# Moving the places where h's two parts and the stacks begin in their SBUF buffers

## The chip, the core and the metric

The kernel runs on one core of one Trainium2 chip. The metric is the device time of one execution in microseconds (us); lower is better. The core has five engines that run their own instruction queues and wait for each other through semaphores: TensorE (PE, with its weight loads shown apart as PEld), VectorE (DVE), ScalarE (ACT), GpSimd (POOL) and SyncE (SP), which here issues the DMAs.

## What is computed

Inputs are `x` of 4 batches x 12416 rows x 128 features, 32 learned rows `inducing`, and three weight matrices of a gated feed-forward layer with 1536 hidden units. The reference, cut to what matters:

```
def mab(q, kv):                       # attention, one head
    a = softmax(scale * q @ kv.T)
    return a @ kv
h   = mab(inducing for each batch, x) # 4 x 32 x 128
y   = mab(x, h)                       # 4 x 12416 x 128
g   = y @ w_gate
out = (g * sigmoid(g)) * (y @ w_val) @ w_out
```

Since y is a weighted mean of 32 rows, y @ w_gate is computed as attention weights times (h @ w_gate), so a contraction over 32 rows takes the place of one over 128.

## The kernel before

The feed-forward part is most of the work. For each batch the rows are cut into 25 column tiles: the first has 512 columns, then come twelve of 512 and twelve of 480. For every column tile 12 tiles t of 128 hidden units follow each other; such a pair of column tile and t is a slot, 300 to a batch. In a slot the kernel does this:

- `front`: two matmuls (L668, L669) multiply the batch's weights `tw` with the column tile's `stack`, a 128-row matrix in which the attention weights stand twice as a high part and twice as a low part, into two PSUM banks `gv`. ACT applies SiLU to one (L671, tile `silu`), DVE multiplies with the other (L676), which gives h, in the SBUF tile `h`, or for t = 1, 5 and 9 in the PSUM bank itself.
- `split`, one slot later: h is rounded to fp32r as `h_hi` (L685; by ACT, for t = 11 by DVE), and the rest `h_lo` = h - h_hi is written (L687; by POOL, for t = 1, 5 and 9 by DVE).
- `back`, some 5 to 10 slots later: three matmuls add h_hi times the low part of w_out (L701), h_hi times its high part (L702) and h_lo times the high part (L703) into the PSUM bank `o`. After t = 11 DVE copies `o` to `ob` (L710) and a DMA writes it out.

So PE's queue repeats L668, L669, L701, L702, L703, one round for each slot. The very first column tile of batch 0 is an exception: its h is one part, and L699 multiplies it. Between the slots stand the steps of the attention of this and the next batch, at slots set by a plan; the whole order is written out in the program.

In the first 65 us or so ACT and POOL also make the weights: L187 (POOL) adds the halves of a weight word, L190 (ACT) rounds w_out to `wo_hi`, L193 (POOL) writes `wo_lo`. These have the same form as L685 and L687.

Where things lie in a partition of SBUF, in the built program before the change: there are 11 buffers for h_hi, 10 for h_lo, 3 for h, 2 for silu, each 2048 bytes long and back to back, and every one begins 32 bytes past a multiple of 2048. The 3 buffers of the stack are also back to back and begin 928 bytes past a multiple of 2048; `wo_hi`, `wo_lo`, `tw` and `wgv_sb` begin 1504 bytes past one. Where L193 and L190 read their operands differs: `tw` lies 1504 bytes past a multiple of 2048, as wo_hi and wo_lo do; the pieces in `s_all` and `xn_sb` lie 1952 past one, 448 bytes off. The remainder of a start by 2048 bytes is called its phase below.

Of the kernel before, what the change touches and what calls it, by code (L numbers as in the profile page):

```python
# [9 lines left out]
F32 = mybir.dt.float32  # L10
F32R = mybir.dt.float32r
# [7 lines left out]
P = 128  # L19
# [13 lines left out]
NF = len(FC)  # L33
W = 32 * max(CH)
WF = 32 * max(FC)
NT = DFF // P
SCALE = 1.0 / math.sqrt(C)


COLS = [(0, 0)] + [(q, j) for q in range(1, NF) for j in range(NG)]  # L40
SLOTS = len(COLS) * NT
NXT = 4
# [66 lines left out]
def induced_set_attention_then_swiglu(ctx: ExitStack, tc: tile.TileContext, xt, xn, ind, wgv, wo, out):  # L109
# [8 lines left out]
    stp = ctx.enter_context(tc.tile_pool(name="stp", bufs=NST))  # L118
# [30 lines left out]
    def wcol(k, t):  # L149
        at = WP * (t // 2) + 2 * P * k + P * (t % 2)  # L150
        return slice(at, at + P)
# [46 lines left out]
    def attention(b, one, xn0=None, xt0=None):  # L198

        st = Batch()  # L200
# [14 lines left out]
        def fblocks(q):  # L215
            return FC0[q], FC0[q] + FC[q]
# [200 lines left out]
        def sl2(b0, b1):  # L417
            return st.s2[:, b0:b1, :]
# [32 lines left out]
        def aT(q):  # L451
            st.at[q] = sgl.tile([P, WF], F32, name="aT")
            nc.vector.transpose(out=st.at[q][:, :32 * FC[q]], in_=sl2(*fblocks(q)).rearrange("p t m -> p (t m)"))

        def a_hi(q, eng=nc.vector.tensor_copy):
            st.ah[q] = sgl.tile([P, WF], F32R, name="a_hi")
            eng(out=st.ah[q][:, :32 * FC[q]], in_=st.at[q][:, :32 * FC[q]])  # L457

        def a_lo(q, eng):
            st.al[q] = sgl.tile([P, WF], F32R, name="a_lo")  # L460
            n = 32 * FC[q]
            eng.tensor_sub(out=st.al[q][:, :n], in0=st.at[q][:, :n], in1=st.ah[q][:, :n].bitcast(F32))  # L462

        def stack(u):
            if u not in st.stack:
                st.stack[u] = stp.tile([P, WF], F32R, name="stack")
            return st.stack[u]

        def spread(u):

            q, j = COLS[u]
            n = 32 * FC[q]
            sk = stack(u)
            for g in range(4):
                src = (st.ah, st.al)[g % 2][q]
                for jj in range(NG) if q == 0 else (j,):
                    c0 = n * jj if q == 0 else 0
                    nc.sync.dma_start(out=sk[32 * g:32 * g + 32, c0:c0 + n].bitcast(F32), in_=src[32 * jj:32 * jj + 32, :n].bitcast(F32))
# [41 lines left out]
        def z7(h):  # L520
            nc.scalar.copy(out=zhalf(stack(0), h), in_=zhalf(st.zps, h))

        def z8(h):
            nc.vector.scalar_tensor_tensor(out=zhalf(stack(0), h), in0=zhalf(stack(0).bitcast(F32), h), scalar=odd, in1=zhalf(st.zps, h), op0=ALU.mult, op1=ALU.add)
# [8 lines left out]
    def post(st, q, eng, base, ready=0):  # L533

        f = st.f
        steps = [(0, lambda: f["sum2"](q)), (1, lambda: f["rec2"](q)), (2, lambda: f["norm2"](q, eng)),
                 (5, lambda: f["aT"](q)), (7, lambda: f["a_hi"](q)), (9, lambda: f["a_lo"](q, eng))]
        tiles = [u for u, (p, j) in enumerate(COLS) if p == q]
        return [(base + d, g) for d, g in steps] + [
            (max(base + 12, ready + NT * (u - NST + 1) + 3), lambda u=u: f["spread"](u)) for u in tiles]  # L540

    def plan(st, p):
# [6 lines left out]
        def clear(slot):  # L549

            while slot % NT in p["TABU"]:
                slot += 1
# [41 lines left out]
        for q in range(NF):  # L594
            first = [u for u, (p, j) in enumerate(COLS) if p == q][0]
            s += post(st, q, nc.gpsimd, SLOTS + NT * (first - NST) + 2, SLOTS)
        return sorted(s, key=lambda x: x[0])
# [53 lines left out]
    hip = ctx.enter_context(tc.tile_pool(name="hip", bufs=BF[2]))  # L651
    lop = ctx.enter_context(tc.tile_pool(name="lop", bufs=BF[3]))
# [5 lines left out]
    def front(st, b, c, t):  # L658
        u = Tile()
        q, j = COLS[c]  # L660
        u.b, u.q, u.j, u.t = b, q, j, t
        n = u.n = WF if q == 0 else 32 * FC[q]

        u.whole = b == 0 and c == 0
        rhs = st.stack[c][:, :n]
        u.g = ps_gv.tile([P, 512], F32, name="gv")
        u.v = ps_gv.tile([P, 512], F32, name="gv")
        nc.tensor.matmul(out=u.g[:, :n], lhsT=st.w[:, wcol(0, t)], rhs=rhs, start=True, stop=True)  # L668
        nc.tensor.matmul(out=u.v[:, :n], lhsT=st.w[:, wcol(1, t)], rhs=rhs, start=True, stop=True)  # L669
        s = sip.tile([P, WF], F32, name="silu")  # L670
        nc.scalar.activation(out=s[:, :n], in_=u.g[:, :n], func=AF.Silu)  # L671
        if u.whole:
            u.h = hip.tile([P, WF], F32, name="h_hi")
        else:
            u.h = u.v if t in DVE_TILES else hp.tile([P, WF], F32, name="h")
        nc.vector.tensor_mul(out=u.h[:, :n], in0=u.v[:, :n], in1=s[:, :n])  # L676
        return u

    def split(u):
        if u.whole:  # L680
            return
        n = u.n
        u.hi = hip.tile([P, WF], F32R, name="h_hi")
        u.lo = lop.tile([P, WF], F32R, name="h_lo")
        (nc.vector.tensor_copy if u.cast_dve else nc.scalar.copy)(out=u.hi[:, :n], in_=u.h[:, :n])  # L685
        eng = nc.vector if u.t in DVE_TILES or u.last else nc.gpsimd
        eng.tensor_sub(out=u.lo[:, :n], in0=u.h[:, :n], in1=u.hi[:, :n].bitcast(F32))  # L687
# [3 lines left out]
    def back(u):  # L691
# [5 lines left out]
        if u.whole:  # L697
            k = t % (WP // P)
            nc.tensor.matmul(out=o[:, :n], lhsT=pieces[f"o{t // (WP // P)}"].w[:, P * k:P * k + P], rhs=u.h[:, :n], start=(t == 0), stop=(t == NT - 1))  # L699
        else:  # L700
            nc.tensor.matmul(out=o[:, :n], lhsT=wo_lo[:, ws], rhs=u.hi[:, :n], start=(t == 0), stop=False)  # L701
            nc.tensor.matmul(out=o[:, :n], lhsT=wo_hi[:, ws], rhs=u.hi[:, :n], start=False, stop=False)  # L702
            nc.tensor.matmul(out=o[:, :n], lhsT=wo_hi[:, ws], rhs=u.lo[:, :n], start=False, stop=(t == NT - 1))  # L703
        if t == NT - 1:
# [11 lines left out]
    for b in range(B):  # L716
# [12 lines left out]
        for slot in range(SLOTS):  # L729
            c, t = slot // NT, slot % NT  # L730
            u = front(cur, b, c, t)
            u.cast_dve = t in CAST
            u.last = b == B - 1 and slot == SLOTS - 1
            if wait:
                split(wait[0])
                pend.append(wait.pop(0))
            wait.append(u)
            if slot in bursts:
                u.cast_dve = True
                split(u)  # L740
                pend.append(wait.pop(0))
            for a in (cur, nxt):
                while a is not None and a.steps and a.steps[0][0] <= slot:
                    a.steps.pop(0)[1]()
            ahead = min(ahead + 1 / RAMP, HI) if nxt is not None and slot < last_burst else max(ahead - 1 / RAMP, SKEW)
            if slot in bursts:
                ahead = SKEW
            while len(pend) + len(wait) > ahead:
                back(pend.pop(0))
# [3 lines left out]
    for u in wait:  # L753
        split(u)
# [39 lines left out]
```

## Time and profile before

| | |
|---|---|
| median of 3 runs | 1501.12 us (1500.82 to 1503.07) |
| the profiled execution: its time, its span | 1499.66 us, 1497.6 us |
| mean granted TensorE clock | 0.999 of full speed |
| busy: PE, PEld, DVE, ACT, POOL | 1475.7, 1166.2, 1214.6, 1283.6, 1208.5 us |

The span runs from the first to the last instruction; 2.1 us of the profiled time lie outside of it. PE's busy time is a union of matmuls that overlap in the record, since they are pipelined and their ends are modelled; the distance from one matmul's start to the next one's start tells the pace.

### The profile page before, as it was taken

Reading aid. Unit: us, or ns where it says so; the run is one execution under the profiler, and the core shown is the slowest. Engines: PE = TensorE matmul, PEld = TensorE weight load, DVE = VectorE, ACT = ScalarE, POOL = GpSimd, SP = SyncE. Lnnn points to the kernel's source line nnn. Section 1 sums busy time; section 2 is a strip of 40 time slices with the busy share of each in tenths; the row PEclk is TensorE's granted clock in tenths of the full one; section 3 lists DMA queues with packets and bytes.
Section 4 is the critical chain, followed back from the end, with each engine's and each line's share of the span. In section 5 each row is a group of like instructions: output and inputs, shape, how many; then the busy total and the mean of one; then the engine's idle time right before and its main releaser. Section 6 shows DMA issues by size and latency. Waiting matters only on the chain.

```text
span 1497.6 us, 24960 instructions
## 1 busy us (share of the span) xinstructions
PE 1475.7 (99%) x7465; PEld 1166.2 (78%) x7465; DVE 1214.6 (81%) x2083; ACT 1283.6 (86%) x2389; POOL 1208.5 (81%) x995
## 2 busy tenths in 40 slices
PE   8899999999999999999999999999999999999999
PEld 5576777788887776788887777678888887888887
DVE  6788778878888778788888878878878878878877
ACT  5787888789898887889989888789898898898897
POOL 1588767878898778788888877978889888888887
PEclk9999999999999999999999999999999999999999
DMA  9026322221133333121114324221111111111110
GB/s 369 23 94 187 135 96 94 79 61 56 40 109 120 122 125 112 46 67 37 40 44 131 125 87 156 78 69 48 41 40 35 38 41 41 33 41 39 41 40 20
DMA packets 50822, 119.80 MB, mean 80 GB/s; under 512 B 11392, under 2 KB 28288, under 8 KB 50688
## 3 DMA queue, kind: packets, MB, share of 16 engines
q1 hardware_dynamic: 50688, 118.22, 24.6%
q8 instruction: 59, 0.97, 0.3%
q14 instruction: 75, 0.61, 0.1%
HBM read 62.87 MB, written 25.43 MB: 59 GB/s over the span
## 4 chain that ended last, share of the span: by engine, by line
PE 87%; POOL 2%; ACT 2%; DVE 1%; issue 1%; DVEq 0%; ACTq 0%; POOLq 0%
PE o L701 17%; PE o L703 17%; PE o L702 16%; PE gv L668 16%; PE gv L669 16%; PE o L257 2%; POOL h_lo L687 2%; PE o L305 1%; ACT h_hi L685 1%; ACT silu L671 1%; POOL s_all L449 1%; DVE h L676 1%; PE gv L406 0%; ACT s_all L289 0%; DVE ob L710 0%
## 5 line engine op out<-in xcount | busy, mean ns | idle before, releaser
L687 POOL TENSOR_TENSOR h_lo<-h,h_hi 128x512 fp32r<-128x512 f32 (+1 forms) x890 | 1109.5, 1270 | 238.8 <-ACT h_hi L685 186.9
L671 ACT ACTIVATE silu<-gv 128x512 f32<-128x512 f32 (+1 forms) x1200 | 704.4, 588 | 127.0 <-PE gv L668 89.6
L676 DVE TENSOR_TENSOR h<-gv,silu 128x512 f32<-128x512 f32 (+1 forms) x891 | 594.3, 668 | 206.8 <-ACT silu L671 162.3
L685 ACT CAST h_hi<-h 128x512 fp32r<-128x512 f32 (+1 forms) x788 | 475.5, 603 | 54.0 <-DVE h L676 47.6
L668 PE MATMUL gv<-stack,tw 128*128 128x512 f32 (+1 forms) x1200 | 469.3, 391 | 1.3 <-ACT h_hi L685 0.8
L701 PE MATMUL o<-h_hi,wo_lo 128*128 128x512 f32 (+1 forms) x1188 | 464.4, 391 | 3.8 <-DVE ob L710 2.1
L703 PE MATMUL o<-h_lo,wo_hi 128*128 128x512 f32 (+1 forms) x1188 | 463.2, 390 | 0.6
L669 PE MATMUL gv<-stack,tw 128*128 128x512 f32 (+1 forms) x1200 | 461.8, 385 | 1.8 <-DVE h L676 0.6
L702 PE MATMUL o<-h_hi,wo_hi 128*128 128x512 f32 (+1 forms) x1188 | 458.5, 386 | 0.0
L701 PEld LDWEIGHTS o<-h_hi,wo_lo 128*128 128x128 f32 x1188 | 223.0, 188 | 81.9 <-issue 33.9
L669 PEld LDWEIGHTS gv<-stack,tw 128*128 128x128 f32 x1200 | 225.2, 188 | 53.9 <-ACT silu L671 4.8
L668 PEld LDWEIGHTS gv<-stack,tw 128*128 128x128 f32 x1200 | 225.7, 188 | 50.2 <-issue 3.8
L703 PEld LDWEIGHTS o<-h_lo,wo_hi 128*128 128x128 f32 x1188 | 222.4, 187 | 52.6 <-POOL h_lo L687 12.1
L702 PEld LDWEIGHTS o<-h_hi,wo_hi 128*128 128x128 f32 x1188 | 223.2, 188 | 36.8
L676 DVE TENSOR_TENSOR gv<-gv,silu 128x512 f32<-128x512 f32 (+1 forms) x297 | 201.7, 679 | 46.4 <-ACT silu L671 40.7
L687 DVE TENSOR_TENSOR h_lo<-gv,h_hi 128x512 fp32r<-128x512 f32 (+1 forms) x297 | 197.3, 664 | 1.0
L685 ACT CAST h_hi<-gv 128x512 fp32r<-128x512 f32 (+1 forms) x294 | 167.9, 571 | 4.8 <-DVE gv L676 2.5
L710 DVE COPY ob<-o 128x512 f32<-128x512 f32 (+1 forms) x100 | 66.3, 663 | 1.4 <-PE o L703 1.4
L685 DVE CAST h_hi<-h 128x512 fp32r<-128x512 f32 (+1 forms) x103 | 46.1, 448 | 0.0
L462 POOL TENSOR_TENSOR a_lo<-aT,a_hi 128x512 fp32r<-128x512 f32 (+2 forms) x27 | 36.2, 1340 | 1.5 <-ACT a_hi L457 1.5
L433 POOL TENSOR_TENSOR s_all<-s_all,mx 128x448 f32<-128x448 f32 (+3 forms) x28 | 26.9, 961 | 0.7 <-DVE mx L429 0.7
L449 POOL TENSOR_TENSOR s_all<-s_all,sm 128x512 f32<-128x512 f32 (+2 forms) x27 | 25.9, 958 | 0.4 <-DVE sm L445 0.4
(159 smaller groups left out, 497.4 us busy)
## 6 DMA issues: line engine op xcount, KB each, us to landing
xt_sb<-xt SPq DMA_DIRECT2D x32, 896.0 KB, 5.1
xn_sb<-xn SPq DMA_DIRECT2D x18, 896.0 KB, 6.2
out<-ob SPq DMA_DIRECT2D x52, 256.0 KB, 2.0
out<-ob SPq DMA_DIRECT2D x48, 240.0 KB, 2.0
stack<-a_hi SPq DMA_DIRECT2D x96, 64.0 KB, 2.0
stack<-a_lo SPq DMA_DIRECT2D x96, 64.0 KB, 2.0
stack<-a_hi SPq DMA_DIRECT2D x96, 60.0 KB, 2.0
stack<-a_lo SPq DMA_DIRECT2D x96, 60.0 KB, 2.0
```

What stands on the lines that cost most here:

```text
L449: eng.tensor_mul(out=a, in0=a, in1=st.sm[q][:, :FC[q]].unsqueeze(2).broadcast_to([P, FC[q], M]))
L462: eng.tensor_sub(out=st.al[q][:, :n], in0=st.at[q][:, :n], in1=st.ah[q][:, :n].bitcast(F32))
L668: nc.tensor.matmul(out=u.g[:, :n], lhsT=st.w[:, wcol(0, t)], rhs=rhs, start=True, stop=True)
L669: nc.tensor.matmul(out=u.v[:, :n], lhsT=st.w[:, wcol(1, t)], rhs=rhs, start=True, stop=True)
L671: nc.scalar.activation(out=s[:, :n], in_=u.g[:, :n], func=AF.Silu)
L676: nc.vector.tensor_mul(out=u.h[:, :n], in0=u.v[:, :n], in1=s[:, :n])
L685: (nc.vector.tensor_copy if u.cast_dve else nc.scalar.copy)(out=u.hi[:, :n], in_=u.h[:, :n])
L687: eng.tensor_sub(out=u.lo[:, :n], in0=u.h[:, :n], in1=u.hi[:, :n].bitcast(F32))
L701: nc.tensor.matmul(out=o[:, :n], lhsT=wo_lo[:, ws], rhs=u.hi[:, :n], start=(t == 0), stop=False)
L702: nc.tensor.matmul(out=o[:, :n], lhsT=wo_hi[:, ws], rhs=u.hi[:, :n], start=False, stop=False)
L703: nc.tensor.matmul(out=o[:, :n], lhsT=wo_hi[:, ws], rhs=u.lo[:, :n], start=False, stop=(t == NT - 1))
L710: nc.vector.tensor_copy(out=ob[:, :n], in_=o[:, :n])
```

## The change

The tiles of h_hi and h_lo grow from 512 to 576 columns (from 2048 to 2304 bytes), and h_hi begins at column 0, 16, 32 or 48 of its buffer, h_lo likewise. The pair of offsets is fixed for half a column tile (six slots) and changes with each half: h_hi's offset steps through the four, and after each such round h_lo's goes one on, so that 16 pairs come in turn. The stack's tiles grow from 512 to 528 columns (2112 bytes) and are still used from column 0; since they lie back to back, the three begin 928, 992 and 1056 bytes past a multiple of 2048. Since the buffers of h_hi and h_lo are now 2304 bytes apart, they begin at many phases, and `h`, `silu`, `ob` and some tiles of the attention move too: h and silu begin 224 bytes past a multiple of 2048. All starts remain 32 bytes past a multiple of 64. Every row of the PSUM tiles stays where it was.

On all five engines the instructions of the built program, their order, their sizes and the semaphores that they wait for are those of before; only addresses and the distance between a buffer's partitions' rows differ. The diff, whole:

```diff
@@ -33,6 +33,8 @@
 NF = len(FC)
 W = 32 * max(CH)
 WF = 32 * max(FC)
+STEP = 16
+NP = 4
 NT = DFF // P
 SCALE = 1.0 / math.sqrt(C)
 
@@ -463,7 +465,7 @@
 
         def stack(u):
             if u not in st.stack:
-                st.stack[u] = stp.tile([P, WF], F32R, name="stack")
+                st.stack[u] = stp.tile([P, WF + STEP], F32R, name="stack")[:, :WF]
             return st.stack[u]
 
         def spread(u):
@@ -659,6 +661,9 @@
         u = Tile()
         q, j = COLS[c]
         u.b, u.q, u.j, u.t = b, q, j, t
+
+        k = 2 * (len(COLS) * b + c) + t // (NT // 2)
+        u.at = STEP * (k % NP), STEP * (k // NP % NP)
         n = u.n = WF if q == 0 else 32 * FC[q]
 
         u.whole = b == 0 and c == 0
@@ -670,7 +675,7 @@
         s = sip.tile([P, WF], F32, name="silu")
         nc.scalar.activation(out=s[:, :n], in_=u.g[:, :n], func=AF.Silu)
         if u.whole:
-            u.h = hip.tile([P, WF], F32, name="h_hi")
+            u.h = hip.tile([P, WF + STEP * NP], F32, name="h_hi")[:, :WF]
         else:
             u.h = u.v if t in DVE_TILES else hp.tile([P, WF], F32, name="h")
         nc.vector.tensor_mul(out=u.h[:, :n], in0=u.v[:, :n], in1=s[:, :n])
@@ -680,8 +685,8 @@
         if u.whole:
             return
         n = u.n
-        u.hi = hip.tile([P, WF], F32R, name="h_hi")
-        u.lo = lop.tile([P, WF], F32R, name="h_lo")
+        u.hi = hip.tile([P, WF + STEP * NP], F32R, name="h_hi")[:, u.at[0]:u.at[0] + WF]
+        u.lo = lop.tile([P, WF + STEP * NP], F32R, name="h_lo")[:, u.at[1]:u.at[1] + WF]
         (nc.vector.tensor_copy if u.cast_dve else nc.scalar.copy)(out=u.hi[:, :n], in_=u.h[:, :n])
         eng = nc.vector if u.t in DVE_TILES or u.last else nc.gpsimd
         eng.tensor_sub(out=u.lo[:, :n], in0=u.h[:, :n], in1=u.hi[:, :n].bitcast(F32))
```

## Rows read from the trace of the kernel before

**Rows 1.** The page: busy times, the granted clock, the chain that ended last.

```profile
PE 1475.7 (99%) x7465; PEld 1166.2 (78%) x7465; DVE 1214.6 (81%) x2083; ACT 1283.6 (86%) x2389; POOL 1208.5 (81%) x995
...
PEclk9999999999999999999999999999999999999999
...
PE 87%; POOL 2%; ACT 2%; DVE 1%; issue 1%; DVEq 0%; ACTq 0%; POOLq 0%
PE o L701 17%; PE o L703 17%; PE o L702 16%; PE gv L668 16%; PE gv L669 16%; PE o L257 2%; POOL h_lo L687 2%; PE o L305 1%; ACT h_hi L685 1%; ACT silu L671 1%; POOL s_all L449 1%; DVE h L676 1%; PE gv L406 0%; ACT s_all L289 0%; DVE ob L710 0%
```

**Rows 2.** The timeline of PE in a stretch of 512-column tiles: start, us, instruction.

```profile
1257.68 0.39 PE L668 MATMUL gv<-stack,tw 128*128 128x512 f32 x1
1257.90 0.40 PE L669 MATMUL gv<-stack,tw 128*128 128x512 f32 x1
...
1301.26 0.41 PE L668 MATMUL gv<-stack,tw 128*128 128x512 f32 x1
```

**Rows 3.** The same in a stretch of 480-column tiles.

```profile
1366.91 0.38 PE L668 MATMUL gv<-stack,tw 128*128 128x480 f32 x1
1367.12 0.38 PE L669 MATMUL gv<-stack,tw 128*128 128x480 f32 x1
...
1407.98 0.38 PE L668 MATMUL gv<-stack,tw 128*128 128x480 f32 x1
```

**Rows 4.** Groups of PE from 1257.68 to 1301.26: count | busy us, mean ns.

```profile
L668 PE MATMUL gv<-stack,tw 128*128 128x512 f32 x39 | 15.3, 393 | 0.0
L702 PE MATMUL o<-h_hi,wo_hi 128*128 128x512 f32 x38 | 14.9, 392 | 0.0
L701 PE MATMUL o<-h_hi,wo_lo 128*128 128x512 f32 x38 | 14.9, 391 | 0.0
L669 PE MATMUL gv<-stack,tw 128*128 128x512 f32 x38 | 14.8, 388 | 0.0
```

**Rows 5.** Groups of PE over the whole span, shapes apart: counts, means.

```profile
L668 PE MATMUL gv<-stack,tw 128*128 128x512 f32 x624 | 251.8, 404 | 1.3 <-ACT h_hi L685 0.8 <-DVE h L676 0.3
L701 PE MATMUL o<-h_hi,wo_lo 128*128 128x512 f32 x612 | 246.1, 402 | 3.8 <-DVE ob L710 2.1 <-DVE hn L311 1.7
...
L701 PE MATMUL o<-h_hi,wo_lo 128*128 128x480 f32 x576 | 218.3, 379 | 0.0
...
L668 PE MATMUL gv<-stack,tw 128*128 128x480 f32 x576 | 217.5, 378 | 0.0
```

**Rows 6.** Line L193, which subtracts on POOL: duration ns min/median/max, starts, form.

```profile
L193 POOL TENSOR_TENSOR wo_lo<-s_all,wo_hi x1: 1288/1288/1288, 60.6 to 60.6; 128x512 fp32r<-128x512 f32 x1
L193 POOL TENSOR_TENSOR wo_lo<-tw,wo_hi x1: 1306/1306/1306, 61.8 to 61.8; 128x512 fp32r<-128x512 f32 x1
L193 POOL TENSOR_TENSOR wo_lo<-xn_sb,wo_hi x1: 1288/1288/1288, 63.1 to 63.1; 128x512 fp32r<-128x512 f32 x1
```

**Rows 7.** Line L190, which rounds on ACT: the same columns.

```profile
L190 ACT CAST wo_hi<-s_all x1: 611/611/611, 58.9 to 58.9; 128x512 fp32r<-128x512 f32 x1
L190 ACT CAST wo_hi<-tw x1: 612/612/612, 60.4 to 60.4; 128x512 fp32r<-128x512 f32 x1
L190 ACT CAST wo_hi<-xn_sb x1: 617/617/617, 61.4 to 61.4; 128x512 fp32r<-128x512 f32 x1
```

**Rows 8.** Line L295, a DVE transpose between changing phases: the same columns.

```profile
L295 DVE STREAM_TRANSPOSE eT<-s_all x28: 601/635/647, 17.1 to 914.6; 128x448 f32<-128x448 f32 x24, 128x416 f32<-128x416 f32 x4
```

**Rows 9.** The page's groups of the lines that read or write moved tiles.

```profile
L687 POOL TENSOR_TENSOR h_lo<-h,h_hi 128x512 fp32r<-128x512 f32 (+1 forms) x890 | 1109.5, 1270 | 238.8 <-ACT h_hi L685 186.9
L671 ACT ACTIVATE silu<-gv 128x512 f32<-128x512 f32 (+1 forms) x1200 | 704.4, 588 | 127.0 <-PE gv L668 89.6
L676 DVE TENSOR_TENSOR h<-gv,silu 128x512 f32<-128x512 f32 (+1 forms) x891 | 594.3, 668 | 206.8 <-ACT silu L671 162.3
L685 ACT CAST h_hi<-h 128x512 fp32r<-128x512 f32 (+1 forms) x788 | 475.5, 603 | 54.0 <-DVE h L676 47.6
```

## Prediction

> **What bounds the kernel now.** I read the page first: busy times, then the chain that ended last [rows 1]. The reader is to see two things there. PE is busy in 99% of the span at a granted clock of 9 in all slices (0.999 in the mean, that is its 2.4 GHz level), and the chain runs through PE for 87% of the span, 82% in the five matmul lines of the feed-forward part (17 + 17 + 16 + 16 + 16). POOL's subtraction L687 has 2% of the chain (30 us), ACT's two lines and DVE's product 1% each (15 us apiece). So a change of PE's pace goes almost whole into the time, and a change on another engine only by its small share of the chain.
>
> Next the timeline of PE in two undisturbed stretches, for the pace. Between the first and the last row of [rows 2] stand 190 steps (38 rounds of five matmuls): 1301.26 - 1257.68 = 43.58 us, 229.4 ns a step at 512 columns. In [rows 3] it is again 190 steps: 1407.98 - 1366.91 = 41.07 us, 216.2 ns at 480 columns. At 2.4 GHz the columns alone take 512 / 2.4 = 213.3 and 480 / 2.4 = 200.0 ns. So every matmul takes 16 ns more than its columns (16.1 and 16.2), and this surplus is the same for both widths: it belongs to the instruction and not to the column. The counts are in [rows 5]: L668 and L701 run 624 and 612 times at 512 columns, L669 as L668, L702 and L703 as L701, which makes 2 x 624 + 3 x 612 = 3084; the five lines run 576 times each at 480, which makes 2880. The feed-forward part at that pace is 3084 x 0.2294 + 2880 x 0.2162 = 707.5 + 622.7 = 1330 us of the 1497.6. The rest is the start, the attention's matmuls and stalls.
>
> **The change part by part.** No instruction is removed, added or moved and no wait is new; what remains to be costed is whether an instruction takes longer or shorter when its operands begin elsewhere. For each kind of instruction I look for two rows of one form whose operands lie at different phases.
>
> *Matmuls that read h_hi and h_lo:* 3 x 612 + 3 x 576 = 3564. *Matmuls that read a stack:* 2 x 624 + 2 x 576 = 2400, of which two thirds, 1600, read a buffer whose phase moves (928 stays, 992 and 1056 are new). The trace of before already holds two phases: the stack's 928 and h's 32. If the phase mattered, L668 and L669 would stand apart from L701 and L702. In the stretch of [rows 4] their records last 393 and 388 (mean 390.5) against 391 and 392 (mean 391.5) ns; over the whole span at 480 columns L668 and L701 have 378 and 379 [rows 5]. The ends are modelled, so I take this as a sign and not as a proof, and use the timeline beside it: over the 38 rounds of the stretch (191 rows, of which the first two and the last stand in [rows 2]; the first step there is 0.22) the steps from L668 to L669 sum to 8.73 us and those from L701 to L702 to 8.74, 229.7 against 230.0 ns. There are also many relations to the weights in it: the twelve column positions of wo_hi and wo_lo lie at four phases (128 columns are 512 bytes), and no round of the stretch is out of step. So the difference that two phases make is at most 1 ns by the means and 0.3 by the timeline. The bounds are 1 ns either way on the 5164 moved matmuls: -5.2 to +5.2 us. The value taken is 0, since the nearest rows, the timeline's, differ by less than they are printed to.
>
> *POOL's subtraction* (890 on L687, 1109.5 us [rows 9]). L193 has its very form, 128x512 with an fp32r output. With all three operands at one phase (`tw`) it took 1306 ns; with one operand 448 bytes off (`s_all`, `xn_sb`) 1288 and 1288 [rows 6]. A different phase costs nothing there and may save 18 ns, 1.4%. At full size that would be 890 x 0.018 = 16 us of POOL's time, but POOL stands idle for 238.8 us ahead of these subtractions, mostly for ACT's rounding [rows 9]; on the chain it has 30 us, and 1.4% of that is 0.4 us. Bounds -0.4 and +0.4 us (the same size with the other sign); taken: 0.
>
> *ACT's rounding.* L190 is of the same form: 612 ns at equal phases, 611 and 617 at unequal ones [rows 7], so -0.2 to +0.8%; of 15 us on the chain that is 0.1 us. SiLU reads PSUM and writes one SBUF tile; I give it the same bound, 0.1 us. *DVE:* the transposes L295 go between four buffers and many places in `s_all`, and all last 601 to 647 ns around 635, two widths included [rows 8]; 2% either way of 15 us is 0.3 us. Taken for both: 0.
>
> *The stack's DMAs* write rows that lie 2112 instead of 2048 bytes from the next buffer's; number, size and queue of the transfers stay. Their cover is the slots between their issue and the first use of the stack; I cost them at nothing, and were the cover gone, PE would wait at L668 for a DMA, for which the trace of before shows no row among its groups' releasers [rows 5].
>
> **Sum.** 0 us, with bounds of 5.2 + 0.4 + 0.2 + 0.3 = 6.1 us either way if all fell together. The profiled execution stays at 1499.7 us (a span of 1497.6 and 2.1 outside it). The median of the runs, 1501.1, is 1.5 above it, and I forecast that: 1501.1 us. About 0.2% (3 us) is what a measurement of this kernel can tell from no change; the three runs shown spread over 2.3 us. Its own range, for this case alone, is 1498 to 1504 us.
>
> **Rivals.**
>
> *The 16 ns are a collision that the new starts relieve (faster).* For it speaks that the surplus is there in every matmul, and that h_hi, h_lo, h and silu all lie at one phase in before, so that PE reads and the others write at equal places. The Trainium skill's page "TensorE: Matmul & The Clock Gate", section "Step-by-step: what each phase is for", gives a gap of 512 / 2.4 plus about 2.5 ns, 216 ns, for back-to-back matmuls of 512 columns; this trace disagrees with 229.4, and by the page's figure some 13 ns in each would be avoidable, an estimate of 67 us over the moved 5164. By the rows alone: if the 12 of 16 pairs with unequal offsets lost the 16 ns in the lines that read h_hi and h_lo, the gain would be 0.75 x 3564 x 0.016 = 43 us, 1458 us; with the stacks it could reach 5164 x 0.016 = 83 us, 1418 us. If it were relieved for one pair in 16, 3564 / 16 x 0.016 = 3.6 us, 1497.5 us. It counts as faster from a mean of 3.0 / 5164 = 0.6 ns a matmul. Against it: the stack's reads at phase 928 meet neither the writes of h_hi at the same places nor the weights at the same distance, and they have the surplus as fully as the reads at 32 [rows 2, 4]; and engines that collide by chance would give uneven steps, not 190 even ones at either width [rows 2, 3]. Chance 0.11, most of it for a small gain, around 1496 us.
>
> *Some of the new phases make PE's reads collide (slower).* In before, all reads of h are at phase 32, and perhaps that is a good one. If a quarter of the pairs doubled the surplus in the lines that read h_hi and h_lo, it would cost 3564 / 4 x 0.016 = 14.3 us, 1515 us; it decides from the same 0.6 ns in the mean. For it: only two phases of the moving operand are seen in before, and the change visits many. Against it: those two are 896 bytes apart and alike [rows 4]. Chance 0.11, most of it between 1504 and 1510 us.
>
> *POOL's subtraction slows down where h, h_hi and h_lo stand at different phases, until POOL is the bound (slower).* It has 238.8 / 890 = 268 ns of idle time for each; from 1270 + 268 = 1538 ns on, 21% more, each further ns costs 0.9 us. At 1651 ns (30%) the time would be 1501 + 113 x 0.89 = 1602 us. Against it stand the two rows of L193 with unequal phases, which are shorter, not longer [rows 6]. Chance 0.02.
>
> That the change does not move the starts is no rival: the built program has the new addresses.
>
> **How the numbers follow.** The forecast has 0.76, the relief 0.11, PE's collision 0.11, POOL 0.02. The time predicted is that of the forecast. The range takes in the sum's bounds of 6.1 us, rounded up on the slow side, and with it the smaller half of the first two rivals: 1495 to 1508 us leaves out about 0.1 of the chance. Faster by over 0.2%: 0.11; within: 0.76; slower: 0.11 + 0.02 = 0.13.
>
> **What would show it right or wrong.** In the changed kernel's timeline of PE, steps of 229.4 and 216.2 ns on average in undisturbed stretches, alike for all offset pairs: a relief or a collision would show as six slots that run at another pace than the six before. L687 should stay within 20 ns of 1270 on POOL in the mean, L685 within 6 of 603. The prediction would be wrong if one of the phases not seen so far cost or saved a few ns in each matmul; nothing in before excludes this for phases other than 32 and 928.

## The result and the profile after

The changed kernel took 1510.12 us in the median of 4 runs (1507.45 to 1511.85), the kernel before 1502.09 beside it: a ratio of 1.0051, interval 1.0029 to 1.0073. It is slower by half a per cent, outside the range. One of the runs listed further down, of e4, took 1806.72 us at a granted clock of 0.753; e4's median is that of its other 11 runs.

The page of the changed kernel, with the rows that answer to [rows 1] and [rows 9] (the file is five lines longer there, so L668 to L703 are now L673 to L708):

```profile
PE 1484.3 (99%) x7465; PEld 1168.1 (78%) x7465; DVE 1220.5 (81%) x2083; ACT 1283.5 (85%) x2389; POOL 1210.1 (80%) x995
...
PEclk9999999999999999999999999999999999999999
...
PE o L706 17%; PE o L708 17%; PE gv L673 17%; PE gv L674 17%; PE o L707 16%; PE o L259 2%; POOL h_lo L692 2%; ACT silu L676 1%; PE o L307 1%; DMA work<-wgv 1%; ACT h_hi L690 1%; DMA xt<-xt 1%; DVE h L681 1%; PE o L704 1%; ACT s_all L291 0%
...
L692 POOL TENSOR_TENSOR h_lo<-h,h_hi 128x512 fp32r<-128x512 f32 (+1 forms) x890 | 1112.2, 1274 | 245.1 <-ACT h_hi L690 191.4
L676 ACT ACTIVATE silu<-gv 128x512 f32<-128x512 f32 (+1 forms) x1200 | 704.3, 588 | 133.6 <-PE gv L673 90.4
L681 DVE TENSOR_TENSOR h<-gv,silu 128x512 f32<-128x512 f32 (+1 forms) x891 | 594.4, 668 | 207.4 <-ACT silu L676 132.2
L690 ACT CAST h_hi<-h 128x512 fp32r<-128x512 f32 (+1 forms) x788 | 475.4, 603 | 53.8 <-DVE h L681 47.8
```

In these four groups ACT and DVE take as long for each instruction as before and POOL 4 ns more; POOL stands idle 6 us longer ahead of L692 and ACT 7 us longer ahead of L676. PE's busy time is 8.6 us longer, of a span that is 7.8 us longer (1505.4 against 1497.6). So I went to PE's timeline, at the same two times 190 steps of the program as in [rows 2, 3]:

```profile
1264.25 0.40 PE L673 MATMUL gv<-stack,tw 128*128 128x512 f32 x1
...
1308.25 0.39 PE L673 MATMUL gv<-stack,tw 128*128 128x512 f32 x1
...
1373.91 0.38 PE L673 MATMUL gv<-stack,tw 128*128 128x480 f32 x1
...
1415.29 0.37 PE L673 MATMUL gv<-stack,tw 128*128 128x480 f32 x1
```

190 steps take 44.00 and 41.38 us, 231.6 and 217.8 ns a matmul, where they took 229.4 and 216.2. And the pace is no longer one: it changes with the offsets. In this piece of PE's timeline each row is the first matmul of a round of five:

```profile
1229.29 0.39 PE L673 MATMUL gv<-stack,tw 128*128 128x512 f32 x1
...
1233.90 0.39 PE L673 MATMUL gv<-stack,tw 128*128 128x512 f32 x1
...
1236.21 0.39 PE L673 MATMUL gv<-stack,tw 128*128 128x512 f32 x1
1237.35 0.39 PE L673 MATMUL gv<-stack,tw 128*128 128x512 f32 x1
...
1241.88 0.39 PE L673 MATMUL gv<-stack,tw 128*128 128x512 f32 x1
1243.03 0.39 PE L673 MATMUL gv<-stack,tw 128*128 128x512 f32 x1
...
1245.34 0.39 PE L673 MATMUL gv<-stack,tw 128*128 128x512 f32 x1
```

The four rounds from 1229.29 to 1233.90 take 4.61 us, 230.5 ns a matmul; the five from 1236.21 to 1241.88 take 5.67, 226.8 ns; the two from 1243.03 to 1245.34 take 2.31, 231 ns. What differs between them is where the operands begin. Put as the remainder of the start by 256 bytes for stack, h_hi and h_lo, the first have 224, 160, 160, the second 224, 224, 224 and the third 160, 32, 224. The weights begin at 224 throughout; in the kernel before it was always 160, 32, 32.

To compare kernels I use the **even pace**: over all rounds L668 to L703 of one width that run through without a stall (under 1200 ns at 512 columns, under 1130 at 480), the mean time from one round's start to the next's, over five. It is 229.5 and 216.3 ns before, 231.3 and 217.5 after. On 3084 and 2880 matmuls that is 5.6 + 3.5 = 9.1 us, of which 7.8 to 8.0 arrive. The steps that are stalls hold 28.1 us more than even ones would in the changed kernel, 29.5 in the one before, so no wait was added.

### The profile page after: what moved, and what is told of

It is laid out like the page before. It is cut to its first block, busy times and chain, and to the rows that moved or that the text cites. A ratio compares the mean times of both kernels' runs of the same rounds, so it can differ in the third digit from the quotient of the medians.

```text
span 1505.4 us, 24960 instructions
## 1 busy us (share of the span) xinstructions
PE 1484.3 (99%) x7465; PEld 1168.1 (78%) x7465; DVE 1220.5 (81%) x2083; ACT 1283.5 (85%) x2389; POOL 1210.1 (80%) x995
## 4 chain that ended last, share of the span: by engine, by line
PE 88%; ACT 3%; DVE 2%; POOL 2%; DMA 2%; issue 2%; SPq 0%; DVEq 0%; ACTq 0%; POOLq 0%
PE o L706 17%; PE o L708 17%; PE gv L673 17%; PE gv L674 17%; PE o L707 16%; PE o L259 2%; POOL h_lo L692 2%; ACT silu L676 1%; PE o L307 1%; DMA work<-wgv 1%; ACT h_hi L690 1%; DMA xt<-xt 1%; DVE h L681 1%; PE o L704 1%; ACT s_all L291 0%
## 5 line engine op out<-in xcount | busy, mean ns | idle before, releaser
L692 POOL TENSOR_TENSOR h_lo<-h,h_hi 128x512 fp32r<-128x512 f32 (+1 forms) x890 | 1112.2, 1274 | 245.1 <-ACT h_hi L690 191.4
L676 ACT ACTIVATE silu<-gv 128x512 f32<-128x512 f32 (+1 forms) x1200 | 704.3, 588 | 133.6 <-PE gv L673 90.4
L673 PE MATMUL gv<-stack,tw 128*128 128x512 f32 (+1 forms) x1200 | 471.0, 392 | 1.2 <-ACT h_hi L690 0.8
L674 PE MATMUL gv<-stack,tw 128*128 128x512 f32 (+1 forms) x1200 | 465.4, 388 | 1.8 <-DVE h L681 0.6
L708 PE MATMUL o<-h_lo,wo_hi 128*128 128x512 f32 (+1 forms) x1188 | 462.3, 389 | 0.3
L674 PEld LDWEIGHTS gv<-stack,tw 128*128 128x128 f32 x1200 | 225.3, 188 | 52.9 <-ACT silu L676 4.3
L708 PEld LDWEIGHTS o<-h_lo,wo_hi 128*128 128x128 f32 x1188 | 223.0, 188 | 53.8 <-POOL h_lo L692 11.1
L673 PEld LDWEIGHTS gv<-stack,tw 128*128 128x128 f32 x1200 | 225.4, 188 | 50.6 <-issue 3.8
L692 DVE TENSOR_TENSOR h_lo<-gv,h_hi 128x512 fp32r<-128x512 f32 (+1 forms) x297 | 197.6, 665 | 1.3
L690 DVE CAST h_hi<-h 128x512 fp32r<-128x512 f32 (+1 forms) x103 | 50.1, 487 | 0.0
```

## The experiments

The theory (A): PE's pace depends on where its operands begin within 256 bytes. Rivals: the distance of the buffers or their size does it; PE meets the reads and writes of the other engines; each start has a cost of its own that does not depend on the others. All starts below are remainders by 256 bytes, in the order weights / stack / h_hi and h_lo. "From the pace" is the difference of even pace to before times the counts; the last column is the difference of the medians of runs on the same chip.

| kernel | starts | pace 512, 480 | from the pace, us | ratio, interval | medians, us |
|---|---|---|---|---|---|
| before | 224 / 160 / 32 | 229.5, 216.3 | | | |
| the change | 224 / three / 16 pairs | 231.3, 217.5 | +9.1 | 1.0051, 1.0029 to 1.0073 | +8.0 |
| e1 size only | 224 / 160 / 32 | 229.4, 216.3 | -0.1 | 0.9998, 0.9987 to 1.0009 | -0.2 |
| e9 others moved | 224 / 160 / 32 | 229.5, 216.3 | -0.2 | 1.0005, 0.9993 to 1.0018 | +1.2 |
| e2 | 224 / 224 / 224 | 227.4, 216.7 | -5.2 | 0.9982, 0.9973 to 0.9992 | -2.1 |
| e3 | 224 / 32 / 32 | 229.2, 218.4 | +5.2 | 1.0029, 1.0019 to 1.0039 | +5.9 |
| e4 | 96 / 96 / 96 | 227.4, 216.7 | -5.2 | 0.9981, 0.9972 to 0.9990 | -2.9 |
| e5 | 0 / 0 / 0 | 227.5, 216.7 | -5.1 | 0.9971, 0.9960 to 0.9982 | -5.2 |
| e6 stack alone | 224 / 224 / 32 | 231.8, 217.1 | +9.4 | 1.0102, 1.0086 to 1.0118 | +15.4 |
| e7 weights alone | 96 / 160 / 32 | 229.7, 218.4 | +6.7 | 1.0030, 1.0021 to 1.0040 | +4.1 |
| e8 by width | 224 / 224 / 224 at 512, 160 at 480 | 227.4, 216.1 | -7.1 | 0.9966, 0.9952 to 0.9979 | -4.8 |
| e13 by width | 224 / 224 / 224 at 512, 220 at 480 | 227.4, 214.9 | -10.4 | 0.9952, 0.9939 to 0.9966 | -8.1 |

**e1: the size alone.** Buffers of 576 columns, all starts where they were modulo 256 bytes.

```diff
-        u.hi = hip.tile([P, WF], F32R, name="h_hi")
-        u.lo = lop.tile([P, WF], F32R, name="h_lo")
+        u.hi = hip.tile([P, WF + 64], F32R, name="h_hi")[:, 0:0 + WF]
+        u.lo = lop.tile([P, WF + 64], F32R, name="h_lo")[:, 0:0 + WF]
```

Expected: 

> Only the tiles of h_hi and h_lo grow to 576 columns; both begin at column 0 and the stacks stay, so all starts are at the places modulo 256 bytes that they had before (stack 160 bytes past a multiple of 256, h_hi and h_lo 32). Theory A (PE's pace depends on where its moving operands begin within 256 bytes): the steps stay at 229.4 and 216.2 ns and the time at 1501 us, within 3. Theory B (the distance between the buffers, 2304 instead of 2048 bytes, or the greater footprint, slows PE or the others): 1508 to 1510 us, steps near 231.3 and 217.5 ns.

Its two stretches in PE's timeline:

```profile
1257.99 0.40 PE L668 MATMUL gv<-stack,tw 128*128 128x512 f32 x1
...
1301.57 0.40 PE L668 MATMUL gv<-stack,tw 128*128 128x512 f32 x1
```

43.58 us, to the hundredth what before had. The buffers of h_hi and h_lo now begin at eight places within 2048 bytes, whole multiples of 256 bytes apart, and nothing comes of it: at these starts nothing of h's place beyond its remainder by 256 bytes counts, and the larger buffers cost nothing.

**e2, e3, e4, e5: all three at one place.** A gap ahead of the stacks, offsets for h_hi and h_lo of 32 columns; e4 and e5 also have a gap ahead of the weights.

```diff
+    gap = ctx.enter_context(tc.tile_pool(name="gap", bufs=1))
+    gap.tile([P, 16], F32, name="gap_s")     # e3: 32
     stp = ctx.enter_context(tc.tile_pool(name="stp", bufs=NST))
...
+    const.tile([P, 32], F32, name="gap_w")   # e4; e5: 8; e2, e3: none
     wgv_sb = const.tile([P, 2 * DFF], F32, name="wgv_sb")
...
+        u.hi = hip.tile([P, WF + 64], F32R, name="h_hi")[:, 32:32 + WF]
+        u.lo = lop.tile([P, WF + 64], F32R, name="h_lo")[:, 32:32 + WF]
```

Expected of e2: 

> As the size-only kernel, but stack, h_hi and h_lo all begin 224 bytes past a multiple of 256, where the weights begin too. Theory A: in the changed kernel the rounds with this triple had steps of 226.6 ns at 512 columns; held throughout that is 2.8 ns less than before on 3084 matmuls, 8.6 us; at 480 columns 0 to 3 ns less on 2880, 0 to 8.6 us: 1484 to 1493 us. Theory B: as slow as the size-only kernel. Theory A2 (only that all three are equal counts, not where): the same time as when all three begin at 32.

Expected of e3: 

> Stack, h_hi and h_lo all begin 32 bytes past a multiple of 256; the weights stay at 224. Theory A with A2 (equal starts are what counts): the steps of the kernel with all at 224, 226.6 ns at 512 columns, 1484 to 1493 us. Theory A with A1 (the place relative to the weights, or the place itself, counts): about 230 ns at 512 and 218 at 480 columns, as the few rounds of this triple in the changed kernel had, 1502 to 1508 us.

Expected of e4: 

> Weights, stack, h_hi and h_lo all begin 96 bytes past a multiple of 256: the relations of the kernel with all at 224, another place. If the relation to the weights counts, its steps and its time are those of that kernel (226.6 ns at 512 columns, 1484 to 1493 us); if the place itself counts, they differ by some ns a matmul, and the time lies nearer to 1501 to 1508 us.

Expected of e5: 

> Weights, stack, h_hi and h_lo all begin on a multiple of 256 bytes: the relations of the kernels with all at 224 and all at 96, now aligned. T1 (only the relation of the starts counts): their steps, 227.4 and 216.7 ns a matmul in rounds without a stall, and their time, 1497 to 1499 us. T2 (a start that is no multiple of 64 bytes costs by itself, and all kernels so far had such starts): the surplus over 213.3 and 200 ns falls to a few ns; 13 ns less on 5964 matmuls would be 78 us, about 1420 us.

PE's timeline of e2, then of e3, then of e5, first and last rows of the same stretches:

```profile
1259.70 0.40 PE L670 MATMUL gv<-stack,tw 128*128 128x512 f32 x1
...
1302.79 0.39 PE L670 MATMUL gv<-stack,tw 128*128 128x512 f32 x1
...
1368.18 0.38 PE L670 MATMUL gv<-stack,tw 128*128 128x480 f32 x1
...
1409.35 0.38 PE L670 MATMUL gv<-stack,tw 128*128 128x480 f32 x1
```

```profile
1262.80 0.39 PE L670 MATMUL gv<-stack,tw 128*128 128x512 f32 x1
...
1306.29 0.39 PE L670 MATMUL gv<-stack,tw 128*128 128x512 f32 x1
...
1372.03 0.37 PE L670 MATMUL gv<-stack,tw 128*128 128x480 f32 x1
...
1413.50 0.38 PE L670 MATMUL gv<-stack,tw 128*128 128x480 f32 x1
```

```profile
1253.04 0.40 PE L671 MATMUL gv<-stack,tw 128*128 128x512 f32 x1
...
1296.13 0.39 PE L671 MATMUL gv<-stack,tw 128*128 128x512 f32 x1
```

e2 has 43.09 us over 190 steps, 226.8 ns; e5 the same 43.09; e3 43.49, 228.9. At 480 columns e2 has 41.17 (216.7) and e3 41.47 (218.3). So equal starts are not enough (e3); starts equal to the weights' give the same pace at 224, 96 and 0 (e2, e4, e5): for these what counts is the relation to the weights and not the place. An aligned start gains nothing over the others: the 78 us of the alignment theory are not there. The times, 1496 to 1498 us, miss the 1484 to 1493 expected of e2 and e4, for three reasons: over the whole span the pace at 512 columns is 227.4 and not the 226.6 of the rounds seen; at 480 it rose from 216.3 to 216.7, where I had expected 0 to 3 ns less; and in e2 and e4 less of the gain arrives than the pace gives. Of e2's 5.2 us only 2.1 arrive, and its stalls hold 32.2 us above even steps against 29.5 before; in e5 they hold 29.6, and all of its 5.1 us arrive. Why the stalls differ was not tried; e1, with the pace of before, has 31.0. e2, e4 and e5 have one pace, and their ratios' intervals overlap; they are not told apart.

**e6: the stacks alone; e7: the weights alone.** e6 is e2 with h_hi and h_lo back at 32 (offset 48 in place of 32). e7 has gaps of 32 columns ahead of the weights and of the stacks and offset 0, so that only the weights, and tiles that the feed-forward part doesn't read, move by 128 bytes.

```diff
-        u.hi = hip.tile([P, WF + 64], F32R, name="h_hi")[:, 32:32 + WF]
+        u.hi = hip.tile([P, WF + 64], F32R, name="h_hi")[:, 48:48 + WF]   # e6; h_lo likewise
...
+    const.tile([P, 32], F32, name="gap_w")                                # e7
```

Expected of e6: 

> Only the stacks move, to 224 past a multiple of 256, where the weights begin; h_hi and h_lo begin at 32 as before. T1 (the relation of all operands counts): in the changed kernel the rounds with this triple had 231.6 ns at 512 columns (21 rounds) and 218.2 at 480 (one round): +2.1 x 3084 and +1.9 x 2880, about 12 us, 1508 to 1512 us. T3 (each operand on the weights' place saves its own part): half the gain of the kernel with all at 224, about 1499 us.

Expected of e7: 

> Only the weights move, from 224 to 96 past a multiple of 256 (and with them tiles of the attention's loads); stack at 160, h_hi and h_lo at 32 as before. T1: the steps differ from 229.5 and 216.3 by at least 0.5 ns at one width at least, the sign unknown, since no kernel had this relation. T4 (the weights' place is immaterial, only the moving operands' relation to each other or to the place itself counts): 229.5 and 216.3 ns, 1500 us, within 2.

PE's timeline of e6 at 512 columns, and of e7 at 480:

```profile
1272.85 0.39 PE L670 MATMUL gv<-stack,tw 128*128 128x512 f32 x1
...
1316.93 0.39 PE L670 MATMUL gv<-stack,tw 128*128 128x512 f32 x1
```

```profile
1370.41 0.38 PE L671 MATMUL gv<-stack,tw 128*128 128x480 f32 x1
...
1411.93 0.38 PE L671 MATMUL gv<-stack,tw 128*128 128x480 f32 x1
```

e6 has 44.08 / 190 = 232.0 ns: the stack on the weights' place, alone, is the worst of all kernels, although with h_hi and h_lo there too it is the best. By these two kernels alone, costs of each start by itself could still add up: at 512 columns 2.3 ns more for the stack's move and 4.4 less for h's. The scans below exclude it: with the stack at 224, h has 230.6 ns at 160 and 232.0 at 32 (e11), so 160 is the lower; with the stack at 160, it has 233.4 at 160 (e10) and 229.4 at 32 (the median in before), so 32 is. e7 has 41.52 / 190 = 218.5 ns at 480 columns against 216.2: the moving operands stand still, only the weights moved, and PE's pace changes. At 512 columns it hardly does. e6's time is 6 us above what the even pace gives, and above the 1508 to 1512 us expected; its stalls hold 34.5 us above even steps, 5 more than before, which covers most of it in that profile. Why its stalls grow was not tried.

**e9: the other engines' tiles.** A gap of 16 columns ahead of silu and h, and offset 48 for h_hi and h_lo: PE's operands are at their old places, and h, silu and ob 64 bytes off.

```diff
+    gap.tile([P, 16], F32, name="gap_s")
     sip = ctx.enter_context(tc.tile_pool(name="sip", bufs=BF[0]))
```

Expected: 

> PE's operands stay where they were within 256 bytes (weights 224, stack 160, h_hi and h_lo 32); h, silu and ob, which ACT, POOL and DVE read and write, move from 32 to 96, and the buffers of h_hi and h_lo are 2304 bytes apart. If PE's own two reads (the moving operand and the weights) are what meets: steps of 229.5 and 216.3 ns, 1500 us within 2. If PE meets the other engines' reads and writes: steps off by 0.5 ns or more at one width at least, as with the weights at 96, and a time 2 to 8 us away.

```profile
1260.74 0.40 PE L670 MATMUL gv<-stack,tw 128*128 128x512 f32 x1
...
1304.32 0.40 PE L670 MATMUL gv<-stack,tw 128*128 128x512 f32 x1
```

This is PE's timeline of e9: 43.58 us again. Moving the other engines' tiles by 64 bytes does not change PE's pace. With e7 that leaves PE's own operands.

**e10, e11, e12: scans.** In one run the start changes from column tile to column tile, and each place's even rounds are taken apart. e10 moves stack, h_hi and h_lo together; e11 and e12 move h_hi and h_lo with the stacks at 224.

```diff
+        u.at = 8 * ((c + 3 * b) % 8)                                          # e11
+        u.at = 32 + (-4, -2, -1, 0, 1, 2, 4, 6)[(c + 3 * b) % 8]              # e12
...
+                place[st.b, u] = (32 * (i % 3) + off) % 64                    # e10, off = 8 * (i // 3 % 5)
+                st.stack[u] = stp.tile([P, WF + 32], F32R, name="stack")[:, off:off + WF]
```

Expected of e10: 

> A scan in one run: in each column tile stack, h_hi and h_lo begin at one place modulo 256 bytes, which goes through all eight multiples of 32 from tile to tile; weights stay at 224. If the distance from the weights counts: even rounds at 227.4 (512 columns) and 216.7 (480) where the place is 224, 229.2 and 218.4 where it is 32, and values between 226 and 234 for the others; the rounds of one distance agree within 1 ns. If equality of the three were enough, all eight alike, which the kernel with all at 32 speaks against. The whole time, a mixture: 1500 to 1512 us.

Expected of e11: 

> A scan in one run: stacks at 224 as the weights; h_hi and h_lo together go through all eight multiples of 32 from tile to tile. Known points: 224 gives 227.4 and 216.7 ns a matmul, 160 gives 216.1 at 480 columns, 32 gives 231.8 and 217.1. Where a place below 226.6 at 512 or 216.1 at 480 columns turns up, a faster version follows from it; if none does, the surplus over the columns cannot be lowered by places of 32 bytes below some 13 and 16 ns. The whole time, a mixture: 1500 to 1512 us.

Expected of e12: 

> A scan in one run: stacks at 224 as the weights; h_hi and h_lo together begin at 224 + 4 x (-4, -2, -1, 0, 1, 2, 4, 6) bytes, from tile to tile. If the place counts by the byte: the even rounds of 512 columns have 226.7 ns a matmul at 0 alone and some 228 to 233 at 4 to 24 bytes off, at 480 columns 214 to 219. If only the block of 32 bytes counts in which the start lies: 226.7 at 0 to +24, and what 192 had (232.3) at -4, -8 and -16. Lower than 226.6 anywhere: a better version exists.

The median of the even rounds of each place, over five, in ns (10 to 77 rounds each, from PE's starts in the traces; a round counts where all three operands are at the place):

```
start:                 0      32     64     96     128    160    192    224
e10 all three, 512   233.4  228.8  233.0  232.8  234.4  233.4  233.0  226.6
e10 all three, 480   218.2  218.2  220.0  217.8  220.0  216.0  220.0  216.7
e11 h alone, 512     231.6  232.0  232.0  232.0  232.0  230.6  232.0  226.8
e11 h alone, 480     217.2  218.0  218.6  217.4  218.6  216.0  218.0  216.8

bytes from 224:       -16    -8     -4      0     +4     +8    +16    +24
e12 h alone, 512     231.2  231.2  229.4  226.6  234.8  232.0  232.0  233.0
e12 h alone, 480     216.8  219.8  214.6  216.8  218.6  218.8  217.6  217.4
```

The times of these kernels, one run each, were 1507.2, 1505.7 and 1506.4 us, as expected between 1500 and 1512 where a range was given. At 512 columns there is one low place, the weights' own, and 4 bytes to either side it is gone: 229.4 and 234.8, where 228 to 233 had been expected. So the byte counts, not a block of 32. At 480 columns the lowest median is at another place, 4 bytes before the weights'. Some medians at 480 columns stand for two groups, which the number t of the round's three `back` matmuls separates: in e11 at 0 the rounds of even t have 218.6 ns (31 rounds) and those of odd t 216.0 (33); in e12 at +24 they have 214.0 and 218.0 (33 each). From one t to the next the weights' columns begin 512 bytes further on. So at these places the remainder by 256 bytes is not all that counts: either a longer remainder of the weights' start counts too, or something else that goes with t; no run separates the two. Most places lie above the 229.5 and 216.3 that the kernel before had, which is why a change that goes through many of them loses.

**e8 and e13: a place for each width.** The stacks at 224 and, for h_hi and h_lo, what the earlier runs had as the lowest for either width.

```diff
+        u.at = 32 if q < 4 else 31                                            # e13; e8: 32 and 16
```

Expected of e8: 

> Stack at 224; h_hi and h_lo at 224 in column tiles of 512 and at 160 in those of 480. T1: at 512 columns 227.4 ns as with all at 224; at 480 columns the few rounds of the changed kernel with this triple had 214.6 (four rounds), 1.7 less than before: 2.1 x 3084 + 1.7 x 2880 = 11.4 us less than before, 1488 to 1491 us. If the four rounds were a chance, 216 to 217 ns at 480 columns and 1494 to 1498 us.

Expected of e13: 

> Stacks at 224 as the weights; h_hi and h_lo at 224 in column tiles of 512 and 4 bytes before it, at 220, in those of 480. If the pace is set by the place to the byte, and a scan's rounds carry over to a whole kernel: 227.4 ns at 512 and 215.0 at 480 columns, 2.1 x 3084 + 1.3 x 2880 = 10.2 us less than before, 1489 to 1492 us. If the 215.0 of the scan came from what ran around its tiles: 216 to 217 ns at 480 columns, 1495 to 1498 us, as the kernel with 160 there.

The page's first line of e13 and its two stretches in PE's timeline:

```profile
PE 1466.8 (98%) x7465; PEld 1165.2 (78%) x7465; DVE 1215.3 (82%) x2083; ACT 1282.0 (86%) x2389; POOL 1208.0 (81%) x995
```

```profile
1251.09 0.40 PE L671 MATMUL gv<-stack,tw 128*128 128x512 f32 x1
...
1294.17 0.39 PE L671 MATMUL gv<-stack,tw 128*128 128x512 f32 x1
...
1359.51 0.38 PE L671 MATMUL gv<-stack,tw 128*128 128x480 f32 x1
...
1400.31 0.38 PE L671 MATMUL gv<-stack,tw 128*128 128x480 f32 x1
```

e8's four rounds of 214.6 in the changed kernel were a chance: a whole kernel at that place had 216.1, and its time came out in the second case of the expectation. e13's place, with 56 rounds in the scan, held: 40.80 / 190 = 214.7 ns at 480 columns and 226.7 at 512, and 1491.71 us against 1499.79 beside it, 0.9952. It beats both kernels, with the change's own means: only starts differ.

## Why the prediction was wrong

*What bounds the kernel* was read rightly: a change of PE's pace goes almost whole into the time here (9.1 us from the pace, 8.0 measured), and 1 ns a matmul is about 6 us. In the experiments the rest of the time, the stalls above all, differs from before's by up to 6 us (e6). That the surplus of 16 ns was the same for both widths, and so "belongs to the instruction and not to the column", was an accident of the starts in before: in e2's two stretches it is 13.5 ns at 512 columns and 16.7 at 480.

*The step that failed* is the costing of the matmuls, "So the difference that two phases make is at most 1 ns ... The value taken is 0". I took the stack's 160 (928 modulo 256) and h's 32 as two samples of one cost by place, found them alike, and concluded that the place was immaterial. They were two parts of one sample: the trace held a single combination of weights, stack and h, and the runs show that the pace belongs to the combination (e6 moves the stack alone to the weights' place and is 2.3 ns slower than before at 512 columns; e2 moves h there too and is 2.1 faster). The equal records of [rows 4] could not show this, but the timeline of before could. I compared two of a round's five steps there, L668 to L669 and L701 to L702, and that these two agree was luck. One round of that stretch:

```profile
1280.62 0.39 PE L668 MATMUL gv<-stack,tw 128*128 128x512 f32 x1
1280.85 0.39 PE L669 MATMUL gv<-stack,tw 128*128 128x512 f32 x1
1281.07 0.39 PE L701 MATMUL o<-h_hi,wo_lo 128*128 128x512 f32 x1
1281.30 0.39 PE L702 MATMUL o<-h_hi,wo_hi 128*128 128x512 f32 x1
1281.53 0.39 PE L703 MATMUL o<-h_lo,wo_hi 128*128 128x512 f32 x1
1281.76 0.39 PE L668 MATMUL gv<-stack,tw 128*128 128x512 f32 x1
```

The second step prints as 0.22 us and the others as 0.23. In the mean over the stretch's 38 rounds, from the starts in the trace, the five steps are 229.8, 226.0, 230.0, 229.2 and 231.8 ns: the step from the stack to h is 5.8 ns shorter than the one from h back to the stack. In e2's stretch, where all starts are equal, the five are 226.7 to 226.9. So the rounds of before were even but the steps within them were not, and this was a sign in the trace of before that the starts matter, by several ns. The prediction also said itself that nothing in before excludes a cost of a few ns at other phases; its sum took 0 for it, with bounds of 1 ns.

The measured difference is +1.8 and +1.2 ns, on all 5964 matmuls and not only on the moved 5164, since a stack that stays is read between operands that moved: in the changed kernel's even rounds with the stack at 160, the step from L673 to L674 takes 231.4 ns at 512 columns and 217.3 at 480, where L668 to L669 took 229.9 and 216.0 before. With the measured difference my own sum would have been 1510 us.

*The rival with PE's reads* named the right engine and side at 0.11, but with another mechanism: I priced a doubled surplus for a quarter of the pairs. What the runs show is a surplus of some 13 to 21 ns for nearly every place, and before had one of the lower ones. My argument against it was that even steps exclude collisions by chance. That can hold only for other engines: what the operands of one engine lose to each other can repeat with every round, and the uneven steps of before do repeat (the second is 225 or 226 ns in 37 of the 38 rounds).

*The relief* exists too, but is small: 2.1 ns at 512 and 1.4 at 480 columns in e13, not 16.

*The other engines* were costed rightly: POOL's subtraction 1274 against 1270 ns, ACT's rounding 603 and 603, SiLU 588 and 588; and e9 moved their tiles without a change of PE's pace. DVE's rounding, 103 times, was not costed; its mean rose from 448 to 487 ns, 4 us in all, by a few long ones (the medians are 416 and 417). PE's waits did not grow.

*The page's rule.* The Trainium skill's page "TensorE: Matmul & The Clock Gate", section "Step-by-step: what each phase is for", says that loading the next weights does not take SBUF read bandwidth from the running matmul, since they have independent read ports. Here e7 moved the weights alone, and the pace at 480 columns went from 216.3 to 218.4 ns; so the weights' place does reach the matmuls' pace. Whether it is the two reads that meet, in the memory or on the way, no run here shows. The 216 ns that the section gives for 512 columns were not reached at any place; the lowest median of even rounds was 226.6.

*Still open:* by which mechanism the starts set the pace, why 480 columns have another best place than 512, why t matters at some places, and whether places between the bytes tried, or h_hi and h_lo at different ones, would go lower. The stacks were moved by multiples of 32 bytes only.

## What to carry to other kernels

Where PE streams fp32r matmuls back to back and is the bound, the starts of its operands are a knob worth some per mille (0.2% by e2, 0.5% by e13): begin the moving operands where the weights begin for 512 columns, scan the offsets for other widths, and take an offset for each width. Scan in one run, tile by tile, but believe a place only with some 50 rounds or a whole kernel at it. And two operands that look alike in one profile are one combination, not two samples: before taking a cost as independent of place, look whether the trace holds more than one combination, and compare every step of a round, not two of five.

## What the runs showed of the hardware that was not expected

- PE's step depends on the starts of weights and moving operands, down to 4 bytes: at 512 columns 226.6 ns where all begin at the weights' remainder by 256 bytes, 234.8 with h 4 bytes behind, 229.4 with it 4 bytes ahead (medians in e12).
- Where the starts differ, the five steps of a round differ too: 226.0 to 231.8 ns in before, 226.7 to 226.9 in e2.
- A common shift does nothing (e2, e4 and e5 at 224, 96 and 0: 227.4, 227.4, 227.5 ns at 512 columns), and buffers of h 2304 instead of 2048 bytes apart do nothing (e1).
- The surplus of a matmul over its columns was between 13 and 21 ns at 512 columns and between 15 and 20 at 480 in the medians of the scans, at the full granted clock.
